# Re-ordering every engine's queue of a fused linear-attention and feed-forward kernel, from a plan with new assumptions about DMA

## The chip, the cores and the metric

One NeuronCore of a Trainium2 chip. The time is the device time of one execution in microseconds (us). Medians of several executions are quoted; a ratio is the mean time of one kernel's fast runs over that of the other's fast runs of the same rounds, so it is not quite the ratio of the medians. The profile of an execution covers a "span", from its first to its last instruction, about 1.8 us less than the device time.

Engines: PE is TensorE (matmul), PEld its weight loads, DVE is VectorE, ACT is ScalarE, POOL is GpSimd, SP is SyncE, which here only starts DMA transfers.

## The reference, cut to what matters

```python
# 8 batches x 8 heads, 576 positions, head size 64
q_s = softmax(q, axis=-1)              # over the 64 features
k_s = softmax(k, axis=2)               # over the 576 positions
kv  = einsum('bhsd,bhse->bhde', k_s, v)
att = einsum('bhsd,bhde->bhse', q_s, kv)
x   = att as (4608 tokens, 512)
h   = x @ w_in                         # 512 -> 2048
g   = where(h > 0, h, exp(min(h, 0)) - 1)
out = g @ w_out                        # 2048 -> 512, float32
```

## The kernel before

The program is made as 809 numbered operations ("ops"). Each names its engine and what it reads and writes; the kernel derives all waits from that. A table `ORDER` says in which order each engine runs its ops. It was found ahead of time by a search over a timing model; the kernel holds only its result. The change replaces this table, so the argument below is about ops changing places in a queue.

```python
ORDER = {"pe": "30 28 32 45 43 ...", "act": "3 22 33 23 24 ...", "dve": ..., "gp": ..., "sp": ...}
# Sched.order() puts the five lines together; Sched.emit() adds semaphore waits for every dependence.
```

The work comes in 16 units (a batch and half of its heads; called n = 0 to 15) of attention, and 9 blocks (j = 0 to 8) of 512 tokens of feed-forward:

```python
# attention of unit n (stage1): Q and K arrive by DMA
ACT  exp(q)            DVE  row sums, reciprocals
DVE  QS <- QR * RZQ    # the normalized Q: a tensor_tensor with two SBUF inputs, L383
POOL or ACT  VB <- VR  # V cast to bf16; units 2 and 3 on GpSimd, L371
# QS is transposed: n < 4 on TensorE (L406), n >= 4 by a DMA transpose on SyncE's queue (L422)
PE   K-V product (L458), PE  Q times it (L489), ACT/DVE  evict to XT (L511, L514)

# feed-forward, block j, group g of 8:
PE   8 matmuls 128x512 into one of four PSUM tiles (L545)
ACT  ESB = exp(PS)  (L561);  DVE  or ACT  second step (L578, L572);  DVE  GT = ...  (L580, L574)
PE   out_mm: GT times W2 (L590);  ACT  evict (L607);  SyncE  two stores of 128 KB each (L617)
```

Memory is tight: part of the second GT buffer also serves as staging for the output tiles of block 0.

```python
self.OSB0 = [at(f"OSBX{i}", [128, 512], F32, offset=base + 24576 + 2048 * i) for i in range(4)]
# so GT of block 1, groups 6 and 7, may be written only when the stores of block 0 have landed
```

The softmax here doesn't subtract the row's maximum and nothing guards it: scores larger than these inputs give would overflow.

## Time and profile before

| | before |
|---|---|
| time, 4 executions on the first chip | 303.57 to 303.67, median 303.60 us |
| span of the profiled one (a fifth, 303.79 us) | 302.0 us |
| PE busy | 286.5 us, 95% |
| large matmuls (128x512) | 1152, eight in 1.81 us |

The first two lines of this fence are from the page of the kernel before (busy time, share of the span, number of instructions by engine; then the chain of waits, followed back from the last instruction, as shares of the span). 

```profile
PE 286.5 (95%) x1845; PEld 233.9 (77%) x1845; DVE 188.9 (63%) x244; ACT 183.2 (61%) x213; POOL 20.5 (7%) x31
...
PE 86%; DMA 7%; SPq 2%; issue 1%; ACT 1%; DVE 1%; POOL 0%; POOLq 0%
```

TensorE bounds the kernel: 1152 matmuls at 1.81 us per eight are 261 us. What can be gained is only the time in which TensorE waits. The next fence is from PE's timeline of the kernel before. Columns: start and duration in us, engine, source line, operation and tiles, count, and in brackets the idle time before it and what ended it.

```profile
15.07 1.17 PE L545 MATMUL PS<-XT,W 128*128 128x512 f32 x4 [0.74 <-DVE RZK L467]
...
55.12 2.01 PE L590 MATMUL PS<-W,GT 128*128 128x512 f32 x6 [0.38 <-DVE GT L580]
...
59.89 0.78 PE L458 MATMUL PS<-VB,KR 64*64 64x65 bf16 x72 [0.49 <-ACT KR L359]
...
63.44 2.11 PE L545 MATMUL PS<-XT,W 128*128 128x512 f32 x8 [0.28 <-DVE GT L574]
...
74.50 2.11 PE L545 MATMUL PS<-XT,W 128*128 128x512 f32 x8 [1.03 <-DVE GT L580]
```

The first large matmul starts at 15.07 us, and all the later gaps that this view names lie between 55 and 75 us. The following lines, from the timeline of all engines of the same kernel, show three of their causes.

```profile
53.42 1.95 SPq L422 DMA_TRANSPOSE QT<-QS  x1
...
57.62 1.17 ACT L368 ACTIVATE VB<-VR 128x1152 bf16<-128x1152 f32 x1 [0.56 <-DMA VR<-in_v_dram]
...
60.83 1.36 DVE L383 TENSOR_TENSOR QS<-QR,RZQ 128x1152 f16<-128x1152 f32 x1 [1.18 <-DMA QT<-QS]
...
67.34 1.92 SPq L617 DMA_DIRECT2D out_dram<-OSBX  x3
...
73.22 1.22 DVE L580 TENSOR_TENSOR GT<-ESB,PS 128x1024 fp32r<-128x1024 f32 x1 [2.67 <-DMA out_dram<-OSBX]
```

ScalarE waits for V of unit 5, which lands at 57.6 us; behind it stands the exponential of K, and TensorE's gap at 59.9. VectorE waits 1.18 us for the DMA transpose issued at 53.4, which lands at 60.8; behind that stand a GT and the gap at 63.4. VectorE waits 2.67 us for stores of block 0 that SyncE issued only at 67 to 69 us, and TensorE's gap at 74.5 follows.

To compare kernels I use four moments between which every kernel here does the same TensorE work: the first large matmul, the first matmul of block 1 group 2, the first matmul of block 2 group 0, and the end of the last matmul. They are read from the traces' records.

### The profile page before, as it was taken

How to read it: one execution, taken by the hardware profiler on the slowest of the kernel's cores; microseconds unless marked ns; L12 is line 12 of the kernel's file. 1: busy time of each engine (PE TensorE's matmuls, PEld its weight loads, DVE VectorE, ACT ScalarE, POOL GpSimd, SP SyncE). 2: the span in 40 equal slices, each digit the busy share in tenths (PEclk: the TensorE clock that was granted, in tenths of full speed). 3: DMA queues.
4: the chain of work that ended last, by engine and by line, in shares of the span. 5: the costliest groups of instructions: out<-in, count | busy, mean ns of one | idle time of the engine just before them, and what ended most of it. 6: DMA issues, size and time to landing. Idle time of an engine off the chain costs nothing.

```text
span 302.0 us, 4403 instructions
## 1 busy us (share of the span) xinstructions
PE 286.5 (95%) x1845; PEld 233.9 (77%) x1845; DVE 188.9 (63%) x244; ACT 183.2 (61%) x213; POOL 20.5 (7%) x31
## 2 busy tenths in 40 slices
PE   0799999898999999999999999999999999999995
PEld 0678878676888888888888888888888888888883
DVE  3958935875799785779666767674547256454500
ACT  5858849999968859765972695644445133423411
POOL 0870422000000000000000000000000000000000
PEclk9999999999999999999999999999999999999999
DMA  7999997979487888097349147133003031004035
GB/s 266 393 397 389 388 373 274 200 175 352 117 284 225 210 289 174 0 282 245 91 108 268 65 97 225 41 73 87 2 17 69 0 72 30 22 0 103 3 87 122
DMA packets 35283, 49.96 MB, mean 165 GB/s; under 512 B 16320, under 2 KB 16320, under 8 KB 35264
## 3 DMA queue, kind: packets, MB, share of 16 engines
q1 hardware_dynamic: 29680, 34.09, 41.1%
q0 software_dynamic: 5504, 15.47, 15.9%
q8 instruction: 14, 0.23, 0.3%
q10 hardware_dynamic: 80, 0.13, 0.1%
q14 instruction: 5, 0.04, 0.0%
HBM read 36.70 MB, written 9.44 MB: 153 GB/s over the span
## 4 chain that ended last, share of the span: by engine, by line
PE 86%; DMA 7%; SPq 2%; issue 1%; ACT 1%; DVE 1%; POOL 0%; POOLq 0%
PE PS L590 42%; PE PS L545 40%; DMA VR<-in_v_dram 5%; PE PS L489 2%; DMA out_dram<-OSBX 2%; PE PS L458 2%; SPq L318 1%; SPq L617 1%; POOL KR L318 0%; DVE GT L580 0%; ACT VB L368 0%; ACT KR L359 0%; ACT ESB L561 0%; PE PS L406 0%; DVE VB L371 0%
## 5 line engine op out<-in xcount | busy, mean ns | idle before, releaser
L590 PE MATMUL PS<-W,GT 128*128 128x512 f32 x576 | 141.6, 393 | 0.5 <-DVE GT L580 0.4
L545 PE MATMUL PS<-XT,W 128*128 128x512 f32 x576 | 139.9, 392 | 2.0 <-DVE GT L580 1.0
L545 PEld LDWEIGHTS PS<-XT,W 128*128 128x128 f32 x576 | 106.9, 188 | 25.9 <-DVE GT L580 2.2
L590 PEld LDWEIGHTS PS<-W,GT 128*128 128x128 f32 x576 | 106.5, 188 | 23.1 <-DVE GT L580 0.8
L561 ACT ACTIVATE ESB<-PS 128x1024 f32<-128x1024 f32 x72 | 73.8, 1028 | 73.1 <-PE PS L545 72.6
L578 DVE TENSOR_SCALAR ESB<-ESB 128x1024 f32<-128x1024 f32 x64 | 44.1, 693 | 69.0 <-ACT ESB L561 68.8
L580 DVE TENSOR_TENSOR GT<-ESB,PS 128x1024 fp32r<-128x1024 f32 x64 | 77.5, 1217 | 4.2 <-DMA out_dram<-OSBX 2.7
L607 ACT ACTIVATE OSB<-PS 128x512 f32<-128x512 f32 x32 | 19.2, 599 | 22.6 <-PE PS L590 14.1
L511 ACT ACTIVATE XT<-PS 128x512 fp32r<-128x512 f32 (+6 forms) x32 | 19.4, 609 | 11.2 <-PE PS L489 7.8
L375 DVE TENSOR_REDUCE ZQ<-QR 128x18 f32<-128x1152 f32 x16 | 21.6, 1348 | 7.0 <-ACT QR L355 6.9
L383 DVE TENSOR_TENSOR QS<-QR,RZQ 128x1152 f16<-128x1152 f32 x16 | 21.7, 1356 | 1.6 <-DMA QT<-QS 1.2
L355 ACT ACTIVATE QR<-QR 128x1152 f32<-128x1152 f32 x16 | 18.7, 1169 | 4.0 <-DMA QR<-in_q_dram 3.9
L359 ACT ACTIVATE KR<-KR 128x1152 bf16<-128x1152 f32 x16 | 18.5, 1166 | 1.0 <-DMA KR<-in_k_dram 1.0
L368 ACT ACTIVATE VB<-VR 128x1152 bf16<-128x1152 f32 (+1 forms) x14 | 15.9, 1136 | 1.5 <-DMA VR<-in_v_dram 1.5
L434 ACT ACTIVATE qsT<-QT 128x1152 fp32r<-128x1152 f16 x12 | 13.9, 1161 | 0.3 <-DMA QT<-QS 0.3
L489 PE MATMUL PS<-qsT,MBLK 128*128 128x320 f32 (+5 forms) x64 | 13.9, 304 | 0.0
L489 PEld LDWEIGHTS PS<-qsT,MBLK 128*128 128x128 f32 x64 | 11.7, 190 | 2.7 <-DVE MBLK L471 0.2
L406 PE MATMUL PS<-ID,QS 128*128 128x128 f16 x36 | 3.4, 257 | 8.9 <-DVE QS L383 8.9
L574 DVE SCALAR_TENSOR_TENSOR GT<-PS,ESB 128x1024 fp32r<-128x1024 f32 x8 | 9.8, 1220 | 2.1 <-ACT ESB L572 2.1
L406 PEld LDWEIGHTS PS<-ID,QS 128*128 128x128 f16 x36 | 2.8, 119 | 9.5 <-DVE QS L383 8.9
L471 DVE TENSOR_TENSOR MBLK<-PS,RZK 64x128 fp32r<-64x128 f32 x32 | 9.2, 287 | 0.8
L572 ACT ACTIVATE ESB<-ESB 128x1024 f32<-128x1024 f32 x8 | 8.5, 1061 | 0.2
(28 smaller groups left out, 57.4 us busy)
## 6 DMA issues: line engine op xcount, KB each, us to landing
out_dram<-OSB SPq DMA_DIRECT2D x63, 128.0 KB, 2.4
QR<-in_q_dram SPq DMA_DIRECT2D x12, 576.0 KB, 4.8
KR<-in_k_dram SPq DMA_DIRECT2D x12, 576.0 KB, 6.1
VR<-in_v_dram SPq DMA_DIRECT2D x12, 576.0 KB, 5.1
W<-in_moe_w_out_dram POOLq DMA_DIRECT2D x4, 1024.0 KB, 17.8
QR<-in_q_dram POOLq DMA_DIRECT2D x4, 576.0 KB, 12.6
KR<-in_k_dram POOLq DMA_DIRECT2D x4, 576.0 KB, 10.9
VR<-in_v_dram POOLq DMA_DIRECT2D x4, 576.0 KB, 13.7
```

The costliest lines, as they stand in the source:

```text
L355: S.add("act", t_act(1152, False), lambda e: e.activation(flat(q), flat(q), AF.Exp), key - 3, X=[f"qR{i}"], follow=self.table)
L359: S.add("act", t_act(1152, False), lambda e: e.activation(ek[:, :, :, :].rearrange("p h c d -> p (h c d)"), flat(k), AF.Exp), key - 2, X=[ ...
L375: S.add("dve", t_dve(1152), lambda e: e.tensor_reduce(self.ZQ[i][:, :, :].rearrange("p h c -> p (h c)"), q[:, :, :, :].rearrange("p h c d ...
L383: S.add("dve", t_dve(1152), lambda e: e.tensor_tensor(qso, q[:, :, :, :], rz, ALU.mult), key - 3, R=[f"qR{i}", f"RZQ{i}"], W=[f"QS{self.al ...
L489: last = e.matmul(P[:, y:y + n_], M[:, f, :], T[:, c0:c1, f * 64:f * 64 + 64], start=True, stop=True)
L511: S.add("act", t_act((h1 - h0) * n_, True), lambda e, dst=dst, src=src: e.activation(dst, src, AF.Copy), key, W=W, X=X)
L545: last = e.matmul(P[:, t * 512:(t + 1) * 512], self.W1[:, kc, tt * 128:(tt + 1) * 128], self.XT[:, kc, rc:rc + BLK], start=(kc == 0), stop ...
L561: S.add("act", t_act(1024, True), lambda e: e.activation(esb[:, :], P[:, :], AF.Exp), key, W=[f"E{i}"], X=banks)
L578: S.add("dve", t_dve(1024, 2), lambda e: e.tensor_scalar(esb[:, :], esb[:, :], 1.0, -1.0, ALU.min, ALU.add), key, X=[f"E{i}"])
L580: S.add("dve", t_dve(1024), lambda e: e.tensor_tensor(gt, esb[:, :], P[:, :], ALU.max), key, R=[f"E{i}"], W=gw, X=banks)
L590: last = e.matmul(dst, GT[:, jj, ts * 128:(ts + 1) * 128], self.W2[:, jj, :], start=(jj == 0), stop=(jj == 15))
L607: S.add("act", t_act(512, True), lambda e: e.activation(osb[:, :], src, AF.Copy), key, W=[f"O{i}0", f"O{i}1"], X=[f"b{bk}"])
```

## The change

The intent: solve the order anew with a timing model in which DMA queues share bandwidth and a DMA transpose counts as a long transfer. The work is unchanged. The diff, cut to its core:

```diff
 ORDER = {
     "pe": (
-        "30 28 32 45 43 47 50 67 54 68 70 71 69 72 82 86 93 103 115 90 129 137 130 138 131 128 107 "
+        "30 28 32 45 43 47 50 68 54 67 70 71 69 72 82 86 93 103 115 128 90 129 130 138 137 107 131 "
   ... (the rest of all five lines is replaced in the same way)
-        S.ops[-1].margin = 400 if n < 4 else 1000 if n < 6 else 1500      # loads of Q, K, V
+        S.ops[-1].margin = 300 if n < 4 else 800
-            key - 60, R=[f"QS{self.alt(n)}"], W=["QT"], dma="tq", nbytes=128 * 2304)
-        self.S.ops[-1].packet, self.S.ops[-1].margin = 512, 2000          # DMA transpose
+            key - 60, R=[f"QS{self.alt(n)}"], W=["QT"], dma="tq", nbytes=128 * 4608)
+        self.S.ops[-1].packet, self.S.ops[-1].margin = 512, 500
-            S.ops[-1].packet = 2048                                        # stores
+            S.ops[-1].packet, S.ops[-1].margin = 2048, 300
```

`margin` and `nbytes` are only the model's numbers (one more `nbytes`, of W1, is left out here); the transfers are the same. The model's times also set how many dummy matmuls the kernel puts into TensorE's idle time in the prologue.

## The prediction

> **What bounds the kernel now.** TensorE. The page gives PE 95% busy of a 302.0 us span; the chain of waits is 86% PE. In the timeline eight 128x512 matmuls take 1.81 us, so 1152 need 261 us; the first starts at 15.07. From the PE timeline, TensorE loses after that:
> - 15 to 53 us: about 1 us.
> - 52.8 to 80.1 us: 27.3 us elapse for 96 large matmuls (21.8) and 1.6 of small ones: 3.9 lost. Visible gaps: 0.38 (55.1), 0.49 (59.9), 0.28 (63.4), 1.03 (74.5).
> - 81 us to the end: about 2 us.
> So about 7 us are recoverable, over half in one stage.
>
> **Why that stage stalls.** Late DMA. ACT waits for V until 57.6 us: V of unit 5 is issued at 51.3 and lands at 57.6, beside a Q load issued at 53.0 and a transpose issued at 53.4 that needs 7.4 us to land; undisturbed later transposes take 2.9 to 3.4. (The Trainium skill, "DMA: Bandwidth & Descriptors", section "Issuing engines are not separate DMA queues", says that DMAs of all issuers run on the same 16 engines and interleave; these durations agree.) Then VectorE waits 2.67 us for output stores of block 0 (issued 67.3 to 69.3, behind two loads and a transpose) before it may write GT: PE's 1.03 us gap.
>
> **What the change does.** No instruction of the work is added or removed; all five queues are re-ordered. Matmul order is almost the same to 50 us. The order listing shows:
> - SyncE issues five block-0 stores before or around the first transpose, instead of two; I put the last at 62 to 65 us instead of 69. That removes the 2.67 us wait.
> - GpSimd issues V of unit 5 right after the ACT cast that frees its buffer, and that cast stands earlier in ACT's order. I estimate issue at 47 to 48 us, landing at 52 to 53, clear of SyncE's loads.
> - W2's last quarter is issued behind the GpSimd cast of V (ends near 36 us); it lands near 42.5 instead of 40.95, just as its first matmul comes: some tenths lost at most.
> - Prologue: two evictions come ahead of a cast, 0.2 us lost.
>
> **Cost.** Walking the new orders by hand with the trace's durations (1.81 us per eight matmuls, 1.05 to 1.2 us for ACT and VectorE tiles), blocks reach 52 us level with before, and the stage to 81 us gains about 2.5 us. After that I expect nothing, or a few tenths of new stalls: loads are planned with less reserve. All of the gain is on the critical path, as TensorE is. Net: -2 us.
>
> **Predicted: 301.5 us**, 299.7 to 303.7 eight times in ten. Faster by over 2% (under 297.5) 0.03: it needs nearly all the lost time back. Within 2% 0.95. Slower by over 2% 0.02.
>
> **What would show it right.** The waits of ACT on V (57 us) and of VectorE on the block-0 store gone or under 0.5 us; PE's lost time between 53 and 80 us down by 2 us; busy times unchanged within 1%; first large matmul at 15.0 to 15.4; tail the same.
>
> **What would make it wrong.** Transposes still stretched to 6 to 7 us by loads beside them; W2's last quarter or a V cast late at 43 to 46 us; new waits of ACT on K or V after 80 us, where SyncE holds loads behind a store or transpose whose data is not ready.

## The result

Measured: 302.66 us median (302.01, 302.55, 302.78, 303.36), against 303.60 for before; ratio 0.9969, 95% interval 0.9947 to 0.9992. So the kernel is faster by 0.94 us where 2.1 was forecast. The time lies in the forecast's range; 1.2 us of the forecast gain are missing. (Run again on two chips, it was faster than before by 1.4 and 0.65 us, by the means.)

The profiled execution was the fastest of the four, 302.01, with a span of 300.2. Its page has the same busy times:

```profile
PE 286.4 (95%) x1855; PEld 234.2 (78%) x1855; DVE 189.0 (63%) x244; ACT 182.7 (61%) x213; POOL 20.2 (7%) x31
...
PE 88%; ACT 6%; DMA 3%; DVE 2%; issue 0%; SPq 0%
```

(The ten more PE instructions are dummy matmuls that fill idle time in the prologue.) PE's timeline of the changed kernel, same columns:

```profile
15.42 1.21 PE L545 MATMUL PS<-XT,W 128*128 128x512 f32 x4
...
53.90 3.94 PE L545 MATMUL PS<-XT,W 128*128 128x512 f32 x16 [0.55 <-ACT OSBX L607]
...
59.13 0.78 PE L458 MATMUL PS<-VB,KR 64*64 64x65 bf16 x72
...
72.48 2.11 PE L545 MATMUL PS<-XT,W 128*128 128x512 f32 x8
```

The gaps from 55 to 75 us are gone, and a new one stands at 53.3 to 53.9 us: TensorE waits for an eviction by ScalarE. The lines for the DMA causes, from the timeline of all engines of the changed kernel:

```profile
53.26 0.58 ACT L607 ACTIVATE OSBX<-PS 128x512 f32<-128x512 f32 x1
...
54.65 1.17 ACT L368 ACTIVATE VB<-VR 128x1152 bf16<-128x1152 f32 x1
...
59.78 1.36 DVE L383 TENSOR_TENSOR QS<-QR,RZQ 128x1152 f16<-128x1152 f32 x1
...
71.21 1.22 DVE L580 TENSOR_TENSOR GT<-ESB,PS 128x1024 fp32r<-128x1024 f32 x1
```

V of unit 5 is cast at 54.65 instead of 57.62, and VectorE no longer waits for the transpose or the stores. So those parts of the forecast are right. But the start is later (15.42 for 15.07 us), and the eviction at 53.26 is late. Here is the same TensorE work in four stretches, in us, for each profiled execution. It includes further traces of both kernels from the experiments below.

| execution (time) | to first large matmul | to block 1 group 2 | to block 2 group 0 | to last matmul |
|---|---|---|---|---|
| before (303.79) | 15.07 | 37.70 | 21.73 | 223.93 |
| before, again (305.72) | 15.12 | 39.03 | 22.24 | 223.94 |
| changed (302.01) | 15.42 | 38.47 | 18.59 | 224.17 |
| changed, again (303.12) | 15.68 | 38.99 | 18.68 | 224.39 |
| changed, look (302.95) | 15.64 | 38.82 | 18.78 | 224.33 |
| changed, third (302.94) | 15.65 | 38.82 | 18.59 | 224.49 |
| *forecast, against the first row* | *+0.2* | *-0.2* | *-2.5* | *0* |
| changed, mean of four, against the first row | +0.53 | +1.08 | -3.07 | +0.42 |

The sum of the last row is -1.04 us, close to the measured medians. The third stretch gained even more than forecast; the first two and the last gave two thirds of it back. Only "before (303.79)" and "changed (302.01)" are from the first result; the others ran on other chips. The second stretch of before itself was 37.70 us in one trace and 39.03 in the other, where TensorE waited for weights (0.3 us at 18.0 and 0.63 at 42.9). So +1.08 holds against the first row alone; that the changed order loses time there rests on waits that its traces have and before's traces lack.

### The profile page after: what moved, and what is told of

It reads as the page before. It is cut to its first block, busy times and chain, and to the rows that moved or that the text cites. A ratio compares the mean times of both kernels' runs of the same rounds, so it can differ in the third digit from the quotient of the medians.

```text
span 300.2 us, 4428 instructions
## 1 busy us (share of the span) xinstructions
PE 286.4 (95%) x1855; PEld 234.2 (78%) x1855; DVE 189.0 (63%) x244; ACT 182.7 (61%) x213; POOL 20.2 (7%) x31
## 4 chain that ended last, share of the span: by engine, by line
PE 88%; ACT 6%; DMA 3%; DVE 2%; issue 0%; SPq 0%
PE PS L590 41%; PE PS L545 41%; PE PS L489 3%; PE PS L458 2%; DMA out_dram<-OSB 2%; ACT QR L355 1%; DMA QR<-in_q_dram 1%; ACT ESB L561 1%; PE PS L406 1%; ACT VB L368 1%; ACT KR L359 1%; PE PS L655 1%; ACT OSB L607 1%; DVE QS L383 0%; DVE ZQ L375 0%; ACT XT L511 0%
## 5 line engine op out<-in xcount | busy, mean ns | idle before, releaser
L383 DVE TENSOR_TENSOR QS<-QR,RZQ 128x1152 f16<-128x1152 f32 x16 | 21.7, 1355 | 0.3
L489 PE MATMUL PS<-qsT,MBLK 128*128 128x320 f32 (+5 forms) x64 | 14.0, 305 | 0.3 <-DVE MBLK L471 0.2
L489 PEld LDWEIGHTS PS<-qsT,MBLK 128*128 128x128 f32 x64 | 11.6, 189 | 3.4 <-DVE MBLK L471 0.6
L406 PE MATMUL PS<-ID,QS 128*128 128x128 f16 x36 | 3.2, 243 | 8.9 <-DVE QS L383 8.9
L406 PEld LDWEIGHTS PS<-ID,QS 128*128 128x128 f16 x36 | 2.4, 109 | 9.3 <-DVE QS L383 8.9
```

Source lines behind the costliest of these rows:

```text
L383: S.add("dve", t_dve(1152), lambda e: e.tensor_tensor(qso, q[:, :, :, :], rz, ALU.mult), key - 3, R=[f"qR{i}", f"RZQ{i}"], W=[f"QS{self.al ...
L489: last = e.matmul(P[:, y:y + n_], M[:, f, :], T[:, c0:c1, f * 64:f * 64 + 64], start=True, stop=True)
```

## The experiments

Twelve runs were made, on chips 5, 4 and 9. There, six executions of one kernel lie 0.6 to 2.3 us apart, so a few tenths can't be told from times alone; the traces carry the argument, one execution each.

### 1 and 2. The changed kernel again: after_again, after_look

Edit: none.

> The changed kernel once more, unaltered. Its four executions so far spread over 1.35 us (302.01 to 303.36) where the kernel before spreads over 0.1. Theory A: the new order has the full gain of the forecast (about 1.8 us in the span, as its one profiled execution shows), and in most executions loses 0.5 to 1.4 us again to a wait on DMA that now has no reserve; then the executions spread again from about 302.0 to 303.4 and the trace of a slow one shows one or more PE gaps on a load or transpose that the profiled one lacks. Rival B: the four were chance (first runs on that chip), and these executions lie within 0.2 us of one another near 302.0.

> The same kernel for a second trace. Theory A: another time than the profiled execution's 302.0, with the difference to be found as a wait on DMA after 53 us; B: the same time within 0.2 us.

Measured: after_again 302.27 to 303.29, median 302.89, ratio 0.9954 (0.9928 to 0.998); after_look 302.95. The executions do spread (theory A), but before spreads there too (303.19 to 304.78, and one of 306.26), so the narrow spread of before on the first chip was no property of that kernel. The main gap that the slower executions have was not a load, as I had expected (a small one in after_look was: ScalarE waited 0.33 us for V of unit 5 at 55.7 us). Against the execution of 302.01, the largest single step comes at 36 us. In the fast execution, VectorE's line L383 is the normalized Q of unit 2, GpSimd's line L371 the cast of V of unit 2, PE's L406 the transposes that need that Q (timelines of the three engines):

```profile
34.10 1.36 DVE L383 TENSOR_TENSOR QS<-QR,RZQ 128x1152 f16<-128x1152 f32 x1
...
34.54 1.92 POOL L371 CAST VB<-VR 128x1152 bf16<-128x1152 f32 x1 [15.70 <-DMA VR<-in_v_dram]
...
35.89 0.68 PE L406 MATMUL PS<-ID,QS 128*128 128x128 f16 x9
```

The same lines of after_again:

```profile
34.35 2.25 DVE L383 TENSOR_TENSOR QS<-QR,RZQ 128x1152 f16<-128x1152 f32 x1
...
34.25 1.14 POOL L371 CAST VB<-VR 128x1152 bf16<-128x1152 f32 x1 [15.37 <-DMA VR<-in_v_dram]
...
36.66 0.68 PE L406 MATMUL PS<-ID,QS 128*128 128x128 f16 x9 [0.36 <-DVE QS L383]
```

Whichever starts first keeps its usual time, and the other takes 0.7 to 0.9 us more in these four traces. The Trainium skill, "SBUF — State Buffer", section "SBUF: two separate sides", states that VectorE and GpSimd share a port pair under an exclusive lock, and that a VectorE op with two SBUF inputs takes part when GpSimd's op reads SBUF: the later one "fully blocks". That is this pair of ops, and the numbers agree: the cast ends at 35.39 us, the product 1.21 us later. The blocked time shows as busy time, not as a wait. In three of four traces of the changed kernel the cast came first. In both traces of before, VectorE came first (by 0.15 and 0.17 us), and TensorE reached the transposes only after the product was done (36.43 and 35.31 us in the first).

### 3 to 5. The two DMA causes, one at a time and together: stores_early, v_early, both_early

All on the kernel before:

```diff
  # stores_early: SyncE, the eight stores of block 0 first
- 8 9 10 11 12 13 171 162 187 185 190 164 209 167 168 210 216 161 165 170 200 199
+ 8 9 10 11 12 13 164 165 161 162 167 168 170 171 187 185 190 209 210 216 200 199
  # v_early: ScalarE, the cast 181 that frees V's buffer five places earlier; 179 and 169 move back
- 135 179 166 169 147 154 181 205
+ 135 181 166 179 147 154 169 205
  # both_early: both edits
```

(The expectations say three places; the edit moves the cast by five. 169 is the eviction of block 0's fourth tile.)

> The kernel before with one part of the change: the eight stores of block 0 stand first in SyncE's queue (issued about 43 to 50.5 us), all else as before. Theory: the wait of VectorE on the block-0 stores (2.67 us at 70.5 to 73.2) and PE's 1.03 us gap at 74.5 go, so 1.0 to 1.3 us faster, 302.4. Rival: the gap only moves, since V of unit 5 stays late (57.6 us), and less than 0.4 us is gained.

> The kernel before with the other part: the ScalarE cast that frees V's buffer stands three places earlier (end near 48 us instead of 51), so GpSimd issues V of unit 5 near 48.5 instead of 51.3 us. Theory: V lands at 53 to 55 us instead of 57.6, ScalarE's wait of 0.56 us and PE's gap of 0.49 us at 59.9 go; 0.3 to 0.8 us faster. Rival: the load still lands after 56 us because the queue, not the issue, holds it, and the time stays within 0.2 us.

> The kernel before with both parts at once: block-0 stores first in SyncE's queue, and the ScalarE cast three places earlier. Theory: the two waits stand in series (each alone gained nothing: with the stores early V came later and PE's gap at 60 us grew from 0.49 to 1.4 us; with V early the store wait grew from 2.67 to 3.1 us), so only both together pay: 1.0 to 1.6 us faster than before. Rival: contention between the stores and V eats it again, under 0.4 us gained.

Measured: stores_early median 303.94 (302.3 to 304.3), ratio 0.9976 (0.9943 to 1.001); v_early 304.01, ratio 0.9996 (0.9971 to 1.0022); both_early 303.06 (302.9 to 303.56) beside 303.92 for before, ratio 0.9971 (0.9938 to 1.0004). All three intervals include 1 (of stores_early, two executions were at 302.3 and 302.8 us and four from 303.9), but the traces show the mechanism. From the timeline of stores_early:

```profile
58.81 1.17 ACT L368 ACTIVATE VB<-VR 128x1152 bf16<-128x1152 f32 x1 [1.33 <-DMA VR<-in_v_dram]
...
61.08 0.78 PE L458 MATMUL PS<-VB,KR 64*64 64x65 bf16 x72 [1.39 <-ACT KR L359]
...
74.44 2.02 PE L545 MATMUL PS<-XT,W 128*128 128x512 f32 x8
```

The gap at 74.5 is gone, and that at 60 us grew from 0.49 to 1.39 us: beside the early stores V lands 1.2 us later than in before's trace. In v_early it is the other way about: no gap at 59.9, and the wait for the stores grows from 2.67 to 3.1 us. V landed at 54.96 us there, but ScalarE, whose other ops had become later, came to its cast at 57.55, as late as in before. Each alone shortens the third stretch by 0.3 and 0.1 us only; both together by 0.96 (20.77 for 21.73 us). From the timeline of both_early:

```profile
57.68 1.17 ACT L368 ACTIVATE VB<-VR 128x1152 bf16<-128x1152 f32 x1
...
61.58 1.36 DVE L383 TENSOR_TENSOR QS<-QR,RZQ 128x1152 f16<-128x1152 f32 x1 [1.40 <-DMA QT<-QS]
...
64.19 2.11 PE L545 MATMUL PS<-XT,W 128*128 128x512 f32 x8 [0.97 <-DVE GT L574]
```

The gap at 64.19 is behind the DMA transpose, as the gap at 63.4 was in before. The first line shows that both_early did not bring V forward: V was issued 2.5 us earlier than in before (48.80 for 51.34), took 8.9 us beside the eight stores and landed at 57.66 us, for 57.59. The third stretch is shorter in good part because it begins 0.54 us later (53.31 for 52.77 us); it ends 0.42 us earlier. The cast, now ahead of two evictions to XT, also makes TensorE wait for one of them, 0.34 us at 50.4 us. So the rival of stores_early was right, and more than right: the gap moved, and V came even later. That of v_early had the time right and the reason wrong, as V did land early. That of both_early (contention eats it) was right for V, though the time gained is 0.9 us.

What these runs show, then, is that the early stores take the wait and the gap at 74.5 away. What V alone is worth they do not show. The changed order removes 3.1 us from this stretch. In before's trace the four gaps in it are 2.18 us: 1.03 behind the stores, 0.49 behind V, 0.28 behind the transpose and 0.38 behind no DMA. In the changed kernel all four are gone; there V has three stores beside it instead of eight and landed at 54.6 us. How much each cause is worth was not separated further.

### 6 and 7. Who takes the port first: dve_first, cast_first

The changed kernel with one more dependence, in either direction:

```diff
+        if n == 2:
+            self.cast2.deps[S.ops[-1]] = "raw"     # dve_first: the cast waits for the product
+            S.ops[-1].deps[self.cast2] = "raw"     # cast_first, instead: the product waits for the cast
```

> The changed kernel, but GpSimd's cast of V of unit 2 waits for VectorE's product of Q of unit 2. In one trace of the changed kernel VectorE's product started first (34.09 us) and took 1.36 us, and the span was 300.2; in two others the cast started first and the product took 2.26 and 2.06 us, and the spans were 301.3 and 301.2. Theory: the two exclude each other on the port that VectorE and GpSimd share, and the order of their starts is chance; forced, the product takes 1.36 us in each execution, the transposes of unit 2 start near 35.9 to 36.1 and the kernel gains 0.4 to 0.6 us on the changed one, median near 302.3 on that chip. Rival: the spread comes from something else (first loads), and the median stays at 302.9 within 0.2.

> The changed kernel with the opposite order forced: VectorE's product of Q of unit 2 waits for GpSimd's cast of V. Theory: always the slow case, transposes of unit 2 at 36.5 to 36.8 us, median 0.1 to 0.4 us above the changed kernel (303.0 to 303.3) and 0.6 to 0.9 above the kernel with VectorE first. Rival: equal to the other within 0.2 us.

Timelines of dve_first (source lines are shifted by the edit):

```profile
34.38 1.36 DVE L385 TENSOR_TENSOR QS<-QR,RZQ 128x1152 f16<-128x1152 f32 x1
...
35.81 1.14 POOL L371 CAST VB<-VR 128x1152 bf16<-128x1152 f32 x1 [16.32 <-DVE QS L385]
...
36.20 0.68 PE L410 MATMUL PS<-ID,QS 128*128 128x128 f16 x9
```

and of cast_first:

```profile
34.00 1.14 POOL L371 CAST VB<-VR 128x1152 bf16<-128x1152 f32 x1 [14.86 <-DMA VR<-in_v_dram]
...
35.18 1.36 DVE L385 TENSOR_TENSOR QS<-QR,RZQ 128x1152 f16<-128x1152 f32 x1 [0.54 <-POOL VB L371]
...
36.60 0.62 PE L410 MATMUL PS<-ID,QS 128*128 128x128 f16 x8
```

With an order forced, both ops take 1.36 and 1.14 us (one trace each): the longer durations came from the overlap alone. The times: dve_first median 303.07 (mean 303.15), cast_first 303.91 (mean 303.68), before 303.92; ratios 0.9972 and 0.9996. The difference of the means, 0.5 us, has the expected sign and is somewhat smaller than the 0.6 to 0.9 expected; with executions from 302.4 to 304.4 it is not clear of noise, and the two traces don't show it (38.56 and 38.65 us in the second stretch). dve_first did not come out below the changed kernel either (303.07 here, 302.89 and 303.05 on other chips), so this expectation failed. In its trace TensorE had a gap of 0.6 us at the K-V product at 60 us, behind V of unit 5, which landed at 55.78 us (54.6 to 55.6 in the changed kernel). V was issued at 48.92 us, no later than there (48.6 to 49.4), so it isn't shown that the later cast caused this.

### 8. The late eviction: evict_early

```diff
  # TensorE: the last quarter of block 0's fourth tile (159) two places earlier
- 173 175 172 159 174 233
+ 173 159 175 172 174 233
  # ScalarE: its eviction (169) two places earlier, and four other tiles (120, 135, 181, 179)
- 98 127 120 133 135 163 166 160 181 154 147 179 205 230 231 169 176
+ 98 120 127 135 133 163 166 181 160 179 154 147 205 169 230 231 176
```

> The changed kernel with one stall of its own taken away: the last quarter of the fourth output tile of block 0 stands two places earlier on TensorE and its eviction three places earlier on ScalarE, with three more ScalarE tiles moved into its idle time at 39 to 42 us. Theory: TensorE's wait of 0.55 us at 53.3 (PE idle until the eviction at 53.84) goes and the kernel gains 0.3 to 0.8 us on the changed one. Rival: ScalarE, busy without a gap from 48.5 to 61.9 us, makes TensorE wait the same time a few tiles later, under 0.2 us gained.

Measured: 302.15 to 302.83 in five executions and 304.40 in the sixth; median 302.63, ratio 0.9961 (0.9924 to 0.9998). The profile is of the sixth. PE's timeline of evict_early:

```profile
50.91 6.66 PE L545 MATMUL PS<-XT,W 128*128 128x512 f32 x28
...
59.41 0.78 PE L458 MATMUL PS<-VB,KR 64*64 64x65 bf16 x72 [0.45 <-ACT KR L359]
...
138.15 0.62 PE L489 MATMUL PS<-qsT,MBLK 128*128 128x384 f32 x2 [0.83 <-ACT qsT L434]
```

The wait at 53.3 is gone; 28 matmuls run without a break, and the second stretch is the shortest of the changed family (37.83 us for 38.47 to 38.99). Of these, 38.47 is the one trace in which VectorE took the port first, as it did here; so the eviction cost that stretch about 0.6 us; the rest of the difference to the other three may be the port's. A part came back at once as a wait for ScalarE at 59 us, as the rival said, and no gain in time is shown: the ratio lies among the changed kernel's own, 0.9954 and 0.9979, from other chips. The outlier has its own cause, in ScalarE's timeline:

```profile
135.88 1.17 ACT L359 ACTIVATE KR<-KR 128x1152 bf16<-128x1152 f32 x1 [2.56 <-DMA KR<-in_k_dram]
```

A load of K, late by 2.6 us, held up ScalarE's queue and with it a transposed Q that was ready. I saw this in one execution.

### 9 and 10. A control, and the changed kernel beside it: before_again, after_third

Edit: none.

> The kernel before against itself, as a control, on the chip of the next three. On the first chip its four executions lay within 0.1 us; on two other chips its eleven executions spread from 303.1 to 304.6 with one at 306. Theory: ratio 1.000 within 0.002, spread of about 1 us; its trace loses most of TensorE's time between 55 and 75 us again (3.5 to 4.5 us). Rival: the first chip's narrow spread belongs to this kernel and returns.

> The changed kernel again, beside the control: 0.9 to 1.4 us below it (ratio 0.995 to 0.997). In its trace TensorE's first large matmul is at 15.4 to 15.8 us, it loses 2.2 to 2.9 us between there and 55 us (before: 1.4), 1.0 to 1.3 us from there to 83 us (before: 4.0), and 2.1 to 2.4 us later (before: 2.1).

Measured: before_again median 304.66, ratio to the same kernel in the same rounds 1.0023 (0.9999 to 1.0048). That is the size of the noise: 0.7 us between two means of the same kernel, a little more than I had expected. after_third: median 303.05, ratio 0.9979 (0.9958 to 0.9999), a smaller gain than I had expected, within that noise; its first large matmul, at 15.65 us, is where it was expected. The trace of before_again (305.72 us) shows where before loses in a slow execution:

```profile
42.86 2.12 PE L590 MATMUL PS<-W,GT 128*128 128x512 f32 x8 [0.63 <-DMA W<-in_moe_w_out_dram]
...
75.12 1.22 DVE L580 TENSOR_TENSOR GT<-ESB,PS 128x1024 fp32r<-128x1024 f32 x1 [3.33 <-DMA out_dram<-OSBX]
```

The last quarter of W2 landed at 42.8 instead of 41.0 us. So the waits of before on DMA differ between its two traces, the store wait among them, while in all four traces of after the third stretch is 18.59 to 18.78 us.

### 11 and 12. Taking the losses away: prologue_back, combined

prologue_back is the changed kernel with the prologue's order of before (TensorE, ScalarE, VectorE):

```diff
- pe 47 50 68 54 67 70 71          + pe 47 50 67 54 68 70 71
- act 23 31 24 34 29 44 35 48 55   + act 23 24 31 29 34 35 44 48 55
- dve 42 46 36 49                  + dve 42 36 46 49
```

combined has this, the edits of evict_early and dve_first, and three more:

```diff
- gp 62 64 99 66 65 125            + gp 62 64 66 65 99 125      # loads of W2 and V ahead of the cast
- pe 243 192 244 245               + pe 243 244 192 245
- sp 200 210 171 161 209 168       + sp 200 210 209 171 161 168 # the transpose ahead of two stores
```

> The changed kernel with only the prologue's order taken back to that of the kernel before (two ScalarE evictions behind the casts again, VectorE's cast of V before its eviction, first matmul group as before). Theory: TensorE's first large matmul comes at 15.0 to 15.2 us instead of 15.4 to 15.8 and all after it is earlier by as much: 0.3 to 0.6 us faster than the changed kernel. Rival: a start that is earlier by 0.4 us is lost again at the waits on DMA at 53 to 60 us, which have their own clock; under 0.15 us gained.

> The changed kernel with its own losses taken away together: prologue order as before, early eviction of the fourth tile of block 0, VectorE's product ahead of the GpSimd cast with the W2 and V loads issued before that cast, one output piece ahead of the K-V product on TensorE, and the second transpose issued ahead of two stores. Theory: the three terms that the forecast set too small (start, 15 to 55 us, port) are worth 1.0 to 1.8 us: 0.8 to 1.6 us faster than the changed kernel, 2 us or more below the kernel before. Rival: the loads of V and K of unit 5, which land at 54 to 57 us in any order, set the pace at 59 us and less than 0.4 us is gained.

Measured: prologue_back 302.53 median (mean 302.68; after_third 303.17), ratio to before 0.9954 (0.9932 to 0.9976): 0.5 us under the changed kernel, in the expected range but less than the 0.7 us between the two means of one kernel above. Its profile fell on the slowest of its six executions (303.89), with a start at 15.45 us, not the expected 15.0 to 15.2. But the prologue's matmuls don't run at one pace: the nine transposes (L406) and the pair of matmuls (L489) just ahead took 1.17 and 1.14 us here, and each between 0.67 and 1.20 us in other traces. Of traces at a like pace, the start is 15.45 here and 15.98 in cast_first; 15.12 in before_again and 15.68 in after_again; 14.76 in both_early and 15.42 in the first trace of the changed kernel. So the changed prologue costs 0.5 to 0.7 us (one trace each), and this kernel does take it back. What sets the pace was not looked into. The slow execution's loss is a DMA transpose that landed at 70.7 us (68.7 in the changed kernel's fast execution):

```profile
70.76 1.16 ACT L434 ACTIVATE qsT<-QT 128x1152 fp32r<-128x1152 f16 x1 [1.44 <-DMA QT<-QS]
...
72.36 0.61 PE L489 MATMUL PS<-qsT,MBLK 128*128 128x384 f32 x2 [1.13 <-ACT XT L511]
```

combined: 301.89 to 303.16, median 302.62, mean 302.53, ratio to before 0.9957 (0.9937 to 0.9978). It is 0.64 us under after_third by the means; I had expected 0.8 to 1.6, and 2 us or more under before, which is 1.3. In its trace (301.99 us) the first stretch is 14.85 us, the second 38.02 and the third 19.27 us. PE's timeline:

```profile
50.14 6.68 PE L549 MATMUL PS<-XT,W 128*128 128x512 f32 x28
56.66 2.00 PE L594 MATMUL PS<-W,GT 128*128 128x512 f32 x8
58.65 0.78 PE L462 MATMUL PS<-VB,KR 64*64 64x65 bf16 x72
59.65 2.11 PE L549 MATMUL PS<-XT,W 128*128 128x512 f32 x8 [0.23 <-DVE GT L584]
```

The start and the second stretch are 1.0 us better than in the changed kernel's fast execution, and 0.7 of it is lost again in the third, where TensorE again waits for a GT of VectorE (0.23 us at 59.65). combined is a little better than both kernels by its mean; but the margin to after_third is again of the size of the noise, and against prologue_back there is no difference to speak of.

## Why the prediction was right or wrong, point by point

- **TensorE bounds the kernel, and the stage from 53 to 80 us holds most of the loss.** Right. TensorE's busy time did not change, and the third stretch is where the gain is: -3.1 us where -2.5 was forecast.
- **The wait of VectorE on the block-0 stores and of ScalarE on V go.** Right in all four traces to within 0.3 us, with looser margins than forecast: V was issued at 48.6 to 49.4 us and landed at 54.6 to 55.6 (forecast 47 to 48, and 52 to 53), and the last store of block 0 was issued at 65.7 to 67.3 us (forecast 62 to 65). "Late DMA" is behind 1.80 of the 2.18 us of gaps in before's trace, but of its three parts only the stores' was shown by an experiment.
- **"Walking the new orders by hand ... blocks reach 52 us level with before."** This is the step that failed. The term was put at 0 and measured +1.1 us in the fast execution (53.89 for 52.77 us) and +1.7 to +1.9 in the three others (which ran on other chips, where before's own second trace comes to this point at 54.15). Three things are in it:
  - The prologue, put at 0.2 us and then not counted: 0.35 to 0.61 us against before's first trace, 0.5 to 0.7 between traces at a like pace.
  - The eviction of block 0's fourth tile, behind two ScalarE tiles of block 1: a wait of 0.5 to 0.6 us in every trace of the changed kernel. By my own recollection I had seen this wait in the walk and dropped it because both orders do the same work up to that point. The same work does not mean the same waits. Without it (evict_early) the second stretch fell by about 0.6 us.
  - The port that VectorE and GpSimd share: the product takes 2.06 to 2.25 us instead of 1.36 in three of four traces, and TensorE then loses 0.3 to 0.5 us ahead of the transposes. The walk used fixed durations (1.05 to 1.2 us for ScalarE and VectorE tiles) and did not ask what else ran at that moment, though the trace of before shows the cast of 2.21 us there and 1.15 us for the other unit's cast.
- **"The last quarter of W2 lands near 42.5, some tenths lost at most."** Right: 42.3 to 43.1 us, no wait for it.
- **"After that I expect nothing, or a few tenths of new stalls."** +0.2 to +0.6 us in the last stretch. The forecast named it and gave it no number in the sum.
- **Range and chances.** The result lies in the range. The centre was off by 1.2 us.

By the traces the mechanism of the gain was right; the terms of loss were too small. That the fastest execution (span -1.8 us) comes close to the forecast is partly luck: there too the second stretch was +0.8 us where -0.2 was forecast, and the third -3.1 where -2.5 was. A walk with fixed durations also has no room for a pair of ops whose order changes from execution to execution.

Open: which part of the third stretch's gain comes from V, which from the transpose and which from the order of ScalarE and VectorE; what sets the pace of the prologue's matmuls; whether any of the single losses is worth as much in the kernel's time as in its stretch, since the gains of prologue_back, evict_early and dve_first are within the noise; and how much the port costs in the whole, as the forced orders differ by 0.5 us with noise of that size.

## What to carry to other kernels

When a new order of the same work is judged, add up the waits of each stretch in both orders, and don't let one stretch cancel by the argument that the same work is done. Two late transfers that feed the same stage can hide each other: taking one wait away can make the other transfer later (V by 1.2 us here) or its wait longer (2.67 to 3.1 us). And check in the trace that an edit made to bring a transfer forward did so: in both_early it did not. Check whether a VectorE op with two SBUF inputs runs beside a GpSimd op that reads SBUF (here they started 0.1 to 0.5 us apart); if so, the one that starts later takes longer, here by 0.7 to 1.2 us, and the profile shows the loss as busy time.

## What the Trainium skill lacked or had wrong

- "SBUF — State Buffer" has the exclusive lock of the port pair right (1.36 against 2.06 to 2.25 us for the product, 1.14 against 1.86 to 2.30 us for the cast). The page tells of ops that measure slower under the lock; what it does not say is that the profile counts the blocked time as busy and names no wait for it.
- "DMA: Bandwidth & Descriptors", section "Issuing engines are not separate DMA queues", says that transfers interleave, without a size for the effect on this mix. Here one DMA transpose of a unit took 2.8 to 2.9 us from issue to landing late in the kernel, with little beside it, and 5.3 to 7.9 at 53 to 55 us, beside loads; with eight stores of 128 KB moved ahead, a 576 KB load landed 1.2 us later, and issued 2.5 us earlier beside them it landed no earlier (one trace each).
- I found no page that gives the spread of executions of one kernel. Here the kernel before lay within 0.1 us in four executions on one chip, and over 1.9 to 3.6 us in eleven on each of chips 5, 4 and 9, with an unchanged program.
